# Front of an attention-plus-Fourier kernel: both row groups of a product accumulate into one bank, the upper one 17 products behind

## The chip, the cores and the metric

The kernel runs on one core of a Trainium2 chip. The time is the device time of the core in microseconds (us), from the first to the last instruction of an execution and what lies around it; lower is better. The engines are TensorE (PE, with its weight loads as PEld), VectorE (DVE), ScalarE (ACT), GpSimd (POOL) and SyncE (SP), which here only issues transfers. TensorE writes to PSUM, which has 128 partitions and eight banks of 512 four-byte numbers each; a product of 512 columns fills one bank.

## The reference

For x of 2048 by 512 the kernel gives `g * a + (1 - g) * b`:

```python
g = sigmoid((x * gate_w).sum(-1, keepdims=True))
# a: full attention, 32 heads of 16, softmax over 2048 keys
qkv = x @ wqkv                       # 512 -> 3 * 512
p = softmax(q @ k.T * 16 ** -0.5)
a = concat_heads(p @ v) @ wo
# b: real part of a Fourier transform over both axes
b = dft_seq_re @ (x @ dft_hid_re.T) - dft_seq_im @ (x @ dft_hid_im.T)
```

The weights wqkv and wo are large (64 times 0.05), so the softmax is sharp and the kernel works with operands split into a high part, rounded to the matrix format, and a low part, the rest. A product is then three products of parts: high by high, high by low, low by high.

## The kernel before

The program has two stages, and each writes its own order of instructions by hand; no scheduler moves them.

**The front** (about the first 365 us) makes five sets of products of x: q, k, v (with wqkv) and the real and imaginary parts of the transform over the hidden axis (called wr and wi after their weights). Each set has 16 output blocks of 128 by 512, so there are 80 blocks. `products` (L301 to L307) runs the 12 products of a block: four slices of 128 of the contracted axis, each with the three products of parts. `halves_of` (L185 to L189) issues a product as two matmuls of 64 rows, one on the lower and one on the upper half of TensorE's rows (the row groups); they run side by side and write to two banks. A block thus ends with two banks, whose sum is the result. The order of blocks is: q and k in turn, for the first 128 columns with one block of q beside them (blocks 0 to 8), the rest of q, the rest of k (to block 31), v (32 to 47), wr (48 to 63), wi (64 to 79).

`project_t` (L368) closes a block of q or k: ScalarE copies the first bank to `tx` (L380); while the scans have not begun, VectorE adds the second bank to it, later ScalarE copies the second bank too (L384) and GpSimd adds the two. Then ScalarE makes the high part `eh`, GpSimd subtracts it to make the low part `el` (both under L245, the line of the helper that runs due work), and SyncE stores both. `project_s` (L399) closes a block of v, wr or wi: ScalarE copies both banks (L406, L407), and GpSimd adds them (L478 for v, L502 for wr and wi, whose sums are stored).

Between the products stand **scans**: the kernel needs the row maxima of the scores of 16 pairs of heads, and the front does the first five pairs, 64 scans each. A scan is two matmuls of 48 rows (one on each row group), each into a bank of its own. The 64 scans of the first pair are plain: VectorE reduces each bank (L298). The 256 scans of the other four are folded (`scan_folded`, L150 to L165): of two adjacent blocks of keys, ScalarE takes the rectified first (L162) and VectorE adds the second and reduces (L164, a custom instruction and a short read of its accumulator). The second matmul of a folded scan is issued one scan later than the first.

Pace and due work hang on a count of slots, one slot per product. `beside` (L255) is called after each product: it raises the count, runs whatever `after(n, ...)` has put down for this slot, and issues scans by a running sum: 3.9 products for each plain scan, `FOLD_PACE` = 2.08 for each folded one. The scans begin 62 slots after block 8 has been issued (slot 170 of 960), when eight loads, put down from 22 slots after block 8, have brought the first pair's rows back from memory.

Eight banks serve this: four tags in two pairs for the blocks (x0, x1, y0, y1; before the scans the first blocks use the scan banks too), four for the scans (d0, k0 on the lower row group, d1, k1 on the upper; d for even scans, k for odd). A bank is reused when its reader is done.

**The main stage** (the rest) runs attention, the transform over the sequence axis and the remaining scans on eight other tags, in macro steps written out in `ORDERS`. The change does not touch it.

Of the kernel before, what the change touches and what calls it, by code (L numbers as in the profile page):

```python
# [10 lines left out]
F32 = mybir.dt.float32  # L11
# [7 lines left out]
P = 128  # L19
# [18 lines left out]
FOLD_PACE = 2.08  # L38
# [3 lines left out]
OUTM = 234  # L42
SCAN_MACROS = 226
# [14 lines left out]
def build(tc, x, xT, wqkv, wo, wrT, wiT, cr, ci, gate, out):  # L58
    nc = tc.nc
    with ExitStack() as ctx:  # L60
# [87 lines left out]
        fold = [None, None]  # L148

        def scan_folded(n, j, bank):  # L150
# [6 lines left out]
            b, ps = 64 * j, bank(f"{'dk'[c % 2]}{j}")  # L157
            nc.tensor.matmul(ps, qs[b:b + 48, qb * P:(qb + 1) * P], ks[b:b + 48, c * 512:(c + 1) * 512],  # L158
                             start=True, stop=True)
            if c % 2 == 0:  # L160
                fold[j] = cw.tile([P, 512], F32R, tag=("chi", "clo")[j], name="fold").bitcast(F32)
                nc.scalar.activation(fold[j], ps, AF.Relu)  # L162
            else:
                nc.vector.tensor_tensor_reduce(out=fold[j], in0=ps, in1=fold[j], scale=1.0, scalar=-3.0e38,  # L164
                                               op0=ALU.add, op1=ALU.max, accum_out=mx[p][:, j, qb, c // 2:c // 2 + 1])  # L165
# [55 lines left out]
        with ExitStack() as px:  # L221
            psf = px.enter_context(tc.tile_pool(name="psf", bufs=1, space=PSUM, reuse_waits="tile"))
            turns = [1]

            def narrow(tag, name="s"):
                return psf.tile([P, 512], F32, tag=tag, name=name)

            def xy(a=None):
                turns[0] += 1
                a = a or ("x", "y")[turns[0] % 2]  # L230
                return narrow(a + "0", "xy"), narrow(a + "1", "xy")
# [23 lines left out]
            def beside():  # L255
# [6 lines left out]
                while seen[0] < FRONT and pace[1] >= 1.0:  # L262
# [8 lines left out]
                    if n not in FOLDED:  # L271
                        done = scan_plain(n)
                    else:

                        scan_folded(n, 0, narrow)
                        done = behind(n - 1)
# [7 lines left out]
            def behind(n):  # L284
                if n in FOLDED:
                    scan_folded(n, 1, narrow)
                    return n

            def scan_plain(n):
# [4 lines left out]
                for j in range(2):  # L294
                    ps, b = narrow(f"{'dk'[n % 2]}{j}"), 64 * j
                    nc.tensor.matmul(ps, qs[b:b + 48, i // 4 * P:(i // 4 + 1) * P],
                                     ks[b:b + 48, i % 4 * 512:(i % 4 + 1) * 512], start=True, stop=True)
                    nc.vector.tensor_reduce(mx[p][:, j, i // 4, i % 4:i % 4 + 1], ps, axis=AX.X, op=ALU.max)  # L298
                return n

            def products(ps, parts):  # L301
                n = 0
                for lhs, rhs in parts:
                    for a, b in ((0, 0), (0, 1), (1, 0)):
                        halves_of(ps, lhs[a], rhs[b], n == 0, n == 3 * len(parts) - 1)
                        n += 1
                        beside()  # L307
# [10 lines left out]
            def split_operand(s, raw, engine):  # L318
                ah[s], al[s] = block(2 * s), block(2 * s + 1)
                split(ah[s], al[s], raw, engine)  # L320


            if True:
# [44 lines left out]
                def project_t(w, dst, f, c, ps=None):  # L368
                    ps = ps or xy()
                    products(ps, [([w[i][d][:, f * P:(f + 1) * P] for i in range(2)], xs[d, c])  # L370
                                  for d in range(ND)])
                    tx = ep.tile([P, 512], F32, tag="tx", name="tx", bufs=1)
                    folded = dst is k_d and f < 2
                    if folded and c % 2 == 0:
                        s = even[0] = rp.tile([P, 512], F32, tag="raw", name="ke")
                    else:
                        s = ep.tile([P, 512], F32, tag="ty", name="s")
                    hi = ep.tile([P, 512], F32R, tag="eh", name="eh", bufs=3)
                    lo = ep.tile([P, 512], F32R, tag="el", name="el")
                    nc.scalar.copy(tx, ps[0])  # L380
                    if pace[0] is None:
                        after(5, nc.vector.tensor_add, s, ps[1], tx)
                    else:
                        nc.scalar.copy(s, ps[1])  # L384
                        after(5, nc.gpsimd.tensor_add, s, s, tx)
# [6 lines left out]
                    if folded and c % 2:  # L392
                        after(10, fold_keys, f, c - 1, even[0], s)
                    after(9, nc.scalar.copy, hi, s)
                    after(10, nc.gpsimd.tensor_sub, lo, s, hi.bitcast(F32))
                    after(14, store, 0, hi)
                    after(20, store, 1, lo)

                def project_s(w, t, sign, use):  # L399
                    ps = xy()  # L400
                    q = slice((t % 4) * P, (t % 4 + 1) * P)
                    products(ps, [([v[:, q] for v in xs[d, t // 4]], [w[i][d] for i in range(2)])
                                  for d in range(ND)])
                    tx = ep.tile([P, 512], F32, tag="tx", name="tx", bufs=1)
                    ty = ep.tile([P, 512], F32, tag="ty", name="ty")
                    nc.scalar.mul(tx, ps[0], sign)  # L406
                    nc.scalar.mul(ty, ps[1], sign)  # L407
                    after(4, use, t, tx, ty)
# [29 lines left out]
                warm = [narrow("d0", "warm"), narrow("d1", "warm")]  # L438
# [13 lines left out]
                for n, (w, dst, f, c) in enumerate(order):  # L452
                    project_t(w, dst, f, c, xy("kxdykxdy"[n] if n < 8 else None))
                after(22, load_scan_beside, 0)
                after(62, scan_at, PACE)
                for f, c in [(2, 0), (3, 0)] + [(f, c) for f in range(1, ND) for c in range(1, NC)]:
                    project_t(wq, q_d, f, c)
                wv = new_w()
                for n, (f, c) in enumerate([(f, c) for f in range(1, ND) for c in range(NC)]):
                    if n == 1:  # L460
                        load_w(wv, wqkv[:, 1024:1536], 48, nc.gpsimd)
# [3 lines left out]
                wr = new_cw()  # L465
# [599 lines left out]
```

## Time and profile before

| | |
|---|---|
| median of the two runs | 1866.95 us (1866.27 and 1867.63) |
| profiled execution | 1860.47 us, span 1858.6 us |
| granted TensorE clock, mean | 0.99 |
| matmuls | 13640 |
| PE, DVE, ACT, POOL busy | 96%, 72%, 72%, 40% of the span |

The page gives each engine's busy time; the view by windows gives it for stretches of the span, with the number of instructions in brackets; the view of waits says which instruction ended an engine's idle time; the timeline lists instructions in order of time, with merged neighbours and their count. TensorE's matmuls are pipelined: one takes about 0.4 us from its start to its end, but the next starts about 0.23 us after it, so the pitch between starts, not the duration, is its price.

### The profile page before, as it was taken

What the parts mean: (1) busy time and instruction counts of PE and PEld (TensorE: products, weight loads), DVE (VectorE), ACT (ScalarE), POOL (GpSimd) and SP (SyncE); (2) the same over time, 40 slices, a digit from 0 to 9 for tenths busy, and PEclk for the clock granted to TensorE, in tenths of its full rate; (3) what the DMA queues carried; (4) which work ended last, traced back from release to release, by engine and by line L of the source; (5) the groups of instructions that cost most, each with busy time, mean ns of one, the idle gap of its engine ahead of it and who ended that gap; (6) DMA issues with size and microseconds to landing.
All of it is one profiled execution on the core that took longest, in us unless ns stands there. A gap on an engine that the chain in (4) does not pass through costs nothing.

```text
span 1858.6 us, 36455 instructions
## 1 busy us (share of the span) xinstructions
PE 1787.0 (96%) x13640; PEld 1043.2 (56%) x13640; DVE 1334.2 (72%) x2367; ACT 1331.1 (72%) x2583; POOL 752.1 (40%) x878
## 2 busy tenths in 40 slices
PE   8998899899999999999999899999999899999998
PEld 7776677655555555555555455555554455555554
DVE  6797788777777774886877677668876676684334
ACT  5449898877777777666677677776676677767785
POOL 3685433544444455333333334343333344333122
PEclk9999999999999999999999999999999999999999
DMA  8673325653643444334245644342423343515522
GB/s 280 210 234 90 86 84 124 157 136 101 131 109 87 114 119 119 79 73 85 69 89 122 192 92 91 77 98 71 104 67 67 85 88 79 104 50 131 184 51 94
DMA packets 130529, 205.37 MB, mean 110 GB/s; under 512 B 54336, under 2 KB 56880, under 8 KB 123632
## 3 DMA queue, kind: packets, MB, share of 16 engines
q1 hardware_dynamic: 90000, 176.23, 36.8%
q0 software_dynamic: 38496, 19.47, 4.6%
q10 hardware_dynamic: 1856, 7.34, 1.5%
q8 instruction: 107, 1.75, 0.4%
q14 instruction: 70, 0.57, 0.1%
HBM read 136.71 MB, written 65.81 MB: 109 GB/s over the span
## 4 chain that ended last, share of the span: by engine, by line
PE 77%; DVE 6%; ACT 4%; POOL 4%; DMA 3%; issue 3%; DVEq 0%; ACTq 0%; POOLq 0%; SPq 0%
PE pvb L603 24%; PE z L840 20%; PE s L624 15%; PE s L593 13%; PE xy L189 3%; PE s L158 3%; DVE mx L626 3%; DMA lc<-ob 2%; ACT fold L162 2%; POOL el L245 1%; POOL s L245 1%; DVE ob L633 1%; ACT ty L407 1%; ACT tx L406 1%; DVE y L753 1%
## 5 line engine op out<-in xcount | busy, mean ns | idle before, releaser
L626 DVE TENSOR_REDUCE mx<-s 128x1 f32<-128x512 f32 x1408 | 919.1, 686 | 246.5 <-PE s L593 136.2
L581 ACT ACTIVATE e<-s 128x512 f32<-128x512 f32 x1082 | 607.9, 605 | 210.1 <-PE s L593 167.9
L581 ACT ACTIVATE eb<-s 128x512 f32<-128x512 f32 x966 | 550.4, 605 | 208.3 <-PE s L593 163.5
L593 PE MATMUL s<-qs,ks 50*128 50x512 f32 x2048 | 688.5, 420 | 0.7
L840 PE MATMUL z<-b,chi 64*128 64x512 f32 x2060 | 594.6, 405 | 0.0
L624 PE MATMUL s<-ks,qs 48*128 48x512 f32 x1408 | 529.2, 456 | 27.9 <-DVE mx L626 23.4
L603 PE MATMUL pvb<-e,va 128*17 128x512 f32 x2164 | 473.1, 595 | 0.0
L603 PE MATMUL pvb<-eb,va 128*17 128x512 f32 x1932 | 462.4, 595 | 0.0
L593 PEld LDWEIGHTS s<-qs,ks 50*128 50x128 f32 x2048 | 358.1, 187 | 95.0 <-ACT e L581 27.5
L624 PEld LDWEIGHTS s<-ks,qs 48*128 48x128 f32 x1408 | 215.0, 185 | 331.1 <-DVE mx L626 140.7
L840 PEld LDWEIGHTS z<-b,chi 64*128 64x128 f32 x2060 | 333.8, 187 | 22.3
L840 PE MATMUL z<-b,clo 64*128 64x512 f32 x1030 | 342.5, 404 | 0.0
L215 POOL CAST chi<-craw 128x512 fp32r<-128x512 f32 x126 | 77.3, 613 | 434.5 <-PE z L840 341.4
L164 DVE CUSTOM_DVE_ANT_0 fold<-s,fold 128x512 f32<-128x512 f32 x256 | 172.2, 690 | 49.4 <-ACT fold L162 38.3
L840 PEld LDWEIGHTS z<-b,clo 64*128 64x128 f32 x1030 | 177.5, 188 | 10.8
L216 POOL TENSOR_TENSOR clo<-craw,chi 128x512 fp32r<-128x512 f32 x126 | 161.4, 1281 | 44.1 <-PE z L840 32.4
L636 POOL DMA_DIRECT2D lc<-ob x124 | 63.3, 516 | 273.6 <-DVE ob L633 267.6
L162 ACT ACTIVATE fold<-s 128x512 f32<-128x512 f32 x256 | 146.8, 605 | 21.8 <-PE s L158 12.1
L158 PE MATMUL s<-ks,qs 48*128 48x512 f32 x512 | 135.3, 421 | 22.0 <-ACT fold L162 20.6
L603 PEld LDWEIGHTS pvb<-e,va 128*17 128x17 f32 x2164 | 84.5, 97 | 125.2 <-issue 125.2
L603 PEld LDWEIGHTS pvb<-eb,va 128*17 128x17 f32 x1932 | 81.3, 96 | 106.9 <-issue 106.9
L189 PE MATMUL xy<-w,b 64*128 64x512 f32 x768 | 130.4, 395 | 0.0
(121 smaller groups left out, 1562.7 us busy)
## 6 DMA issues: line engine op xcount, KB each, us to landing
craw<-cr SPq DMA_DIRECT2D x64, 256.0 KB
craw<-ci SPq DMA_DIRECT2D x64, 256.0 KB
ks<-k_d SPq DMA_DIRECT2D x56, 256.0 KB
qs<-q_d SPq DMA_DIRECT2D x56, 256.0 KB
ab_d<-ab SPq DMA_DIRECT2D x32, 256.0 KB
y_d<-y SPq DMA_DIRECT2D x32, 256.0 KB
b<-bs_d SPq DMA_DIRECT2D x32, 256.0 KB
ks<-k_d SPq DMA_DIRECT2D x56, 128.0 KB
```

Source lines behind the costliest of these rows:

```text
L158: nc.tensor.matmul(ps, qs[b:b + 48, qb * P:(qb + 1) * P], ks[b:b + 48, c * 512:(c + 1) * 512], start=True, stop=True)
L162: nc.scalar.activation(fold[j], ps, AF.Relu)
L164: nc.vector.tensor_tensor_reduce(out=fold[j], in0=ps, in1=fold[j], scale=1.0, scalar=-3.0e38, op0=ALU.add, op1=ALU.max, accum_out=mx[p][:, ...
L189: nc.tensor.matmul(ps[j], lhs[r], rhs[r], start=first, stop=last)
L215: copy(hi, raw)
L216: sub(lo, raw, hi.bitcast(F32))
L581: nc.scalar.activation(e, ps, AF.Exp, scale=SCALE)
L593: nc.tensor.matmul(ps, ks[b:b + 50, kb * P:(kb + 1) * P], qs[b:b + 50, q0:q0 + 512], start=True, stop=True)
L603: nc.tensor.matmul(pvb[r:r + VC, :], va[:, kb, 2 * p + j, :], es[step][c, j], start=kb == 0, stop=kb == NB - 1, tile_position=(0, r))
L624: nc.tensor.matmul(ps, qs[b:b + 48, qb * P:(qb + 1) * P], ks[b:b + 48, c * 512:(c + 1) * 512], start=True, stop=True)
L626: nc.vector.tensor_reduce(mx[p][:, j, qb, c:c + 1], ps, axis=AX.X, op=ALU.max)
L840: nc.tensor.matmul(ps, pr_.lhs(j), pr_.rhs(j), start=group.count[j] == 1, stop=group.count[j] == group.size)
```

## The change

- A block now takes **one bank**. `products` issues only the matmul on the lower row group and puts the upper one into a list; once the list holds more than `LAG` = 17, `follow` issues the oldest. The upper group thus runs 17 products behind the lower one, into the bank that the lower one has already filled. At the end 17 upper matmuls are issued alone.
- The two groups must not write one bank at the same time. The **first upper matmul of a block waits** for the eviction (by ScalarE or VectorE) of a scan that was issued after the block's last lower matmul. Where no scans run, `mark` issues one: a matmul of 8 columns into a scan bank and a VectorE copy of one column.
- Banks: three for the blocks (p0 to p2), **five for the scans, in a ring**, whichever row group or parity a scan has.
- **One copy per block**. Before the scans begin ScalarE makes the high part straight from the bank and VectorE the low part; afterwards ScalarE copies the bank once and GpSimd makes both parts. For v, wr and wi ScalarE writes the final tile itself, and GpSimd's additions go. `split_operand` makes its high part on GpSimd, no longer on ScalarE.
- `FOLD_PACE` goes from 2.08 to 1.95 products per folded scan. The loads of the first pair start 30 slots (before: 22) after block 8, the scans 66 slots (62). Some buffers of weights are taken and split at other blocks.

Over the front this leaves ScalarE 106 instructions fewer (546 to 440) and GpSimd 48 fewer (152 to 104); VectorE has 18 short copies more and one addition fewer; TensorE 18 short matmuls more.

```diff
-FOLD_PACE = 2.08
+FOLD_PACE = 1.95
+LAG = 17
...
-            b, ps = 64 * j, bank(f"{'dk'[c % 2]}{j}")
+            b, ps = 64 * j, bank()
...
+            def product_bank():
+                turns[0] += 1
+                return psf.tile([P, 512], F32, tag=f"p{turns[0] % 3}", name="xy")
+            def scan_bank():
+                singles[0] += 1
+                return psf.tile([P, 512], F32, tag=f"s{singles[0] % 5}", name="s")
...
+            def mark(lhs, rhs):
+                ps = scan_bank()
+                issued[0] += 1
+                nc.tensor.matmul(ps[:, 0:8], lhs[0:64], rhs[0:64, 0:8], start=True, stop=True)
+                return nc.vector.tensor_copy(junk, ps[:, 0:1])
+            def follow():
+                ps, lhs, rhs, last, close = behind_.pop(0)
+                if ps.name in ends:
+                    at = ends.pop(ps.name)
+                    later = [ins for n, ins in marks if n > at]
+                    if not later:
+                        later = [mark(lhs, rhs)]
+                ins = nc.tensor.matmul(ps, lhs[64:P], rhs[64:P], start=False, stop=last)
+                if ps.name in starts:
+                    starts.remove(ps.name)
+                    if later:
+                        tc.add_manual_dep(ins.ins, later[0].ins.name, mybir.DependencyInfo(
+                            mybir.DependencyClass.Sync, mybir.DependencyReason.DATA), reason="row groups share a bank")
+                if last:
+                    close(ps)
-            def products(ps, parts):
-                n = 0
-                for lhs, rhs in parts:
-                    for a, b in ((0, 0), (0, 1), (1, 0)):
-                        halves_of(ps, lhs[a], rhs[b], n == 0, n == 3 * len(parts) - 1)
-                        n += 1
-                        beside()
+            def products(parts, close):
+                ps = product_bank()
+                pairs = [(lhs[a], rhs[b]) for lhs, rhs in parts for a, b in ((0, 0), (0, 1), (1, 0))]
+                for n, (lhs, rhs) in enumerate(pairs):
+                    nc.tensor.matmul(ps, lhs[0:64], rhs[0:64], start=n == 0, stop=False)
+                    issued[0] += 1
+                    if n == len(pairs) - 1:
+                        ends[ps.name] = issued[0]
+                        starts.add(ps.name)
+                        marks[:] = marks[-8:]
+                        if pace[0] is None or seen[0] >= FRONT:
+                            seen_by(mark(lhs, rhs))
+                    behind_.append((ps, lhs, rhs, n == len(pairs) - 1, close))
+                    if len(behind_) > LAG:
+                        follow()
+                    beside()
...
-                nc.scalar.copy(tx, ps[0])
-                if pace[0] is None:
-                    after(5, nc.vector.tensor_add, s, ps[1], tx)
-                else:
-                    nc.scalar.copy(s, ps[1])
-                    after(5, nc.gpsimd.tensor_add, s, s, tx)
+                    early = pace[0] is None
+                    if early:
+                        nc.scalar.copy(hi, ps)
+                        nc.vector.tensor_sub(lo, ps, hi.bitcast(F32))
+                    if not early or folded:
+                        nc.scalar.copy(s, ps)
+                    if not early:
+                        after(5, nc.gpsimd.tensor_copy, hi, s)
+                        after(6, nc.gpsimd.tensor_sub, lo, s, hi.bitcast(F32))
...
-                nc.scalar.mul(tx, ps[0], sign)
-                nc.scalar.mul(ty, ps[1], sign)
-                after(4, use, t, tx, ty)
+                    products(..., lambda ps: use(t, ps))
...
-                nc.gpsimd.tensor_add(va[:, t, :, 0:DH], tx..., ty...)
+                nc.scalar.copy(va[:, t, :, 0:DH], ps.rearrange("p (h e) -> p h e", e=DH))
...
-                        nc.gpsimd.tensor_add(ab, tx, ty)
-                        after(7, nc.sync.dma_start, ab_d[i][t], ab)
+                        nc.scalar.mul(ab, ps, (1.0, -1.0)[i])
+                        after(4, nc.sync.dma_start, ab_d[i][t], ab)
...
-                after(22, load_scan_beside, 0)
-                after(62, scan_at, PACE)
+                after(30, load_scan_beside, 0)
+                after(66, scan_at, PACE)
...
+                while behind_:
+                    follow()
+                    beside()
```

99 lines of the change are left out of this document (47 added, 52 removed).

## The prediction

> **What bounds the kernel now.** I read the page's busy shares first (they average over unlike stages), then the windows by stage (us from the start of the span; span of the window, then busy time and, in brackets, instructions of PE, PEld, DVE, ACT, POOL; then clock, DMA share and GB/s).
>
> ```profile
> 0.00:59.20 59.20, 49.50 (x367) 42.83 (x368) 32.95 (x52) 32.29 (x63) 22.97 (x23) 0.94 0.85 280
> 59.20:137.00 77.80, 77.79 (x622) 61.86 (x624) 75.00 (x125) 34.98 (x64) 60.57 (x48) 0.98 0.62 208
> 137.00:208.30 71.30, 60.00 (x466) 44.68 (x462) 52.89 (x157) 63.71 (x131) 39.43 (x32) 1.00 0.31 85
> 208.30:286.30 78.00, 72.95 (x572) 56.74 (x568) 63.09 (x193) 70.44 (x136) 28.06 (x22) 1.00 0.33 97
> 286.30:365.30 79.00, 73.33 (x564) 56.69 (x562) 62.40 (x189) 70.79 (x134) 33.21 (x26) 1.00 0.58 146
> 365.30:373.50 8.20, 5.52 (x31) 3.79 (x28) 6.22 (x12) 5.65 (x12) 4.87 (x5) 0.79 0.52 168
> 373.50:1858.60 1485.10, 1447.94 (x11034) 776.62 (x11032) 1041.68 (x1646) 1053.20 (x2047) 562.95 (x724) 0.99 0.41 98
> ```
>
> The rows are: products alone; plain scans; folded scans beside v (with the end of k), wr and wi; the passage to the main stage; the main stage. The last is untouched and TensorE is busy in 97.5% of it, so what the front saves comes off the end. In the folded stage ScalarE is busiest (about 90%), TensorE is not full. Who makes it wait, and how many scans a window holds (DVE, ACT), say the waits from 137.0 to 365.3 and the windows for the tile `fold`:
>
> ```profile
> PEld s L158 <- ACT fold L162: 39.0, 48, 1.6
> PEld s L158 <- DVE mx L164: 12.0, 54, 0.9
> ...
> DVE fold L164 <- ACT fold L162: 38.3, 41, 1.8
> ```
> ```profile
> 137.00:208.30 71.30, 49.48 (x73) 42.49 (x75) 1.00 0.31 85
> 208.30:286.30 78.00, 61.79 (x93) 52.87 (x93) 1.00 0.33 97
> 286.30:365.30 79.00, 60.86 (x92) 51.48 (x90) 1.00 0.58 146
> ```
>
> TensorE waits for a bank that ScalarE has not emptied, and VectorE waits for ScalarE as well. The timeline shows why:
>
> ```profile
> 208.75 0.59 ACT L406 ACTIVATE tx<-xy 128x512 f32<-128x512 f32 x1
> 209.22 0.61 ACT L407 ACTIVATE ty<-xy 128x512 f32<-128x512 f32 x1
> 209.70 0.64 ACT L475 ACTIVATE xg<-xg 128x512 f32<-128x512 f32 x1
> ...
> 210.31 2.29 ACT L162 ACTIVATE fold<-s 128x512 f32<-128x512 f32 x4
> ```
>
> The copies of a block (and in v's blocks a gate sum) stand together in ScalarE's queue: 0.47 + 0.48 + 0.61 = 1.56 us by the starts, in which no scan bank comes free.
>
> **Prices.** TensorE and VectorE, in a folded stretch, in the plain stage, and VectorE's two kinds of scan:
>
> ```profile
> 241.55 0.43 PE L158 MATMUL s<-ks,qs 48*128 48x512 f32 x2
> ...
> 242.29 0.40 PE L158 MATMUL s<-ks,qs 48*128 48x512 f32 x2
> ...
> 245.35 0.50 PE L158 MATMUL s<-ks,qs 48*128 48x512 f32 x1 [0.33 <-ACT fold L162]
> ```
> ```profile
> 65.28 0.60 PE L296 MATMUL s<-ks,qs 48*128 48x512 f32 x2
> 65.52 1.30 PE L189 MATMUL xy<-b,w 64*128 64x512 f32 x8
> 66.45 0.59 PE L296 MATMUL s<-ks,qs 48*128 48x512 f32 x2
> ```
> ```profile
> 83.73 8.45 DVE L298 TENSOR_REDUCE mx<-s 128x1 f32<-128x512 f32 x14
> ```
> ```profile
> 245.32 0.69 DVE L164 CUSTOM_DVE_ANT_0 fold<-s,fold 128x512 f32<-128x512 f32 x1 [0.86 <-ACT fold L162]
> 245.94 0.08 DVE L164 DVE_READ_ACCUMULATOR2_ANT mx<- 128x1 f32 x1
> 245.94 0.69 DVE L164 CUSTOM_DVE_ANT_0 fold<-s,fold 128x512 f32<-128x512 f32 x1
> ```
>
> Five pairs of matmuls (four products and a scan) take 66.45 - 65.28 = 1.17 us, so a pair (one on each row group) is 0.234 us; three pairs at 241.55 take 0.74, the same within 5%. A plain reduce is (8.45 - 0.69) / 13 = 0.597 us, a folded one 0.62 when its data is there.
>
> **The change, part by part.**
>
> *Folded stage.* Before, a block has 12 / 2.08 = 5.77 scans and costs TensorE 17.77 x 0.234 = 4.16 us, a scan 3.08 x 0.234 = 0.721. Measured: 71.3 / 74 = 0.963 us a scan beside v, 78.0 / 93 = 0.839 beside wr, and beside wi, where the last scan comes 2 us before the end, 77.0 / 91 = 0.846. The stalls are 1.40, 0.68 and 0.72 us a block. ScalarE's burst is 1.56 us beside v and 0.95 beside wr, so what the banks absorb is 0.16 to 0.27; I take 0.2. (Beside wi ten more casts stand on ScalarE, apart from the burst; the change moves them to GpSimd, busy for 33 of 79 us there.) Two things change. The burst loses a copy: 0.48 + 0.61 = 1.09 beside v, 0.48 beside wr and wi; GpSimd's additions, which came behind the copies, go too. And a bank comes back later: before every second scan, 2 x 0.721 = 1.44 us, in the ring after five scan matmuls, 2.5 scans of 2.95 x 0.234 = 0.690, so 1.73; 0.29 more, so 0.5 us is absorbed. Stall: 0.6 a block beside v, none beside wr and wi. At 1.95 a block has 6.15 scans and costs 18.15 x 0.234 = 4.25 us. The 256 scans span 499 products, 41.6 blocks: 12.7 up to the end of v, 28.9 after. Sum 12.7 x 4.85 + 28.9 x 4.25 = 184.4 us. Before it is 363.3 - 136.9, from the first and last start of its weight loads:
>
> ```profile
> L158 PEld LDWEIGHTS s<-ks,qs x512: 182/183/186, 136.9 to 363.3; 48*128 48x128 f32 x171
> ```
>
> 226.4 us, so **-42.0**. Bounds: no stall 41.6 x 4.25 = 177; nothing absorbed beyond 0.2, 12.7 x 5.14 + 28.9 x 4.53 = 196. I stand between, since both the burst and the ring are counted from rows. VectorE is not next: 256 x 0.62 = 159 us.
>
> *The wait of the first upper matmul.* It is new: the eviction of a scan issued after the block's last lower matmul. Queued behind it on TensorE is everything. Six products lie between, and in the folded stage three scans, six matmuls; the sixth needs the bank of the first in a ring of five anyway. So the wait adds about nothing to the ring's; taken at 0 here. In the plain stage only three scan matmuls lie between, and VectorE is the bound: 2 x 0.597 = 1.194 us a scan against TensorE's 4.9 x 0.234 = 1.15. After the wait two or three reduces are still queued (1.2 to 1.8 us), and the next scan comes after at most 3.9 products (0.9 us) and a matmul (0.4). From both sides: nothing, or one reduce (0.6) a block; I take 0.1 for 21 blocks, nearer to nothing for that queue.
>
> *Plain stage.* 64 x 1.194 = 76.4, with the 2.1 us of that wait 78.5, against 136.9 - 59.2 = 77.7: **+0.8** (-1.3 to +11).
>
> *Before the scans.* The stage ends on the first pair's loads, and GpSimd waited for a store before it could write `el` again:
>
> ```profile
> 59.21 0.60 PE L296 MATMUL s<-ks,qs 48*128 48x512 f32 x1 [3.93 <-DMA qs<-q_d]
> ```
> ```profile
> 44.79 0.65 SPq L124 DMA_DIRECT2D ks<-k_d  x1
> ...
> 52.10 0.42 SPq L124 DMA_DIRECT2D qs<-q_d  x1
> ```
> ```profile
> POOL el L245 <- DMA q_d<-el: 12.3, 3, 4.5
> ```
>
> Block 8 ends 17 slots later, but is split straight from the bank and stored 9 to 12 slots after, so its last store moves from slot 128 to 137 and the loads, on SP's queue behind it, by 8 slots: 8 x 0.23 = **+1.8 us**; TensorE, which waited 3.9 us for them, comes to the first scan four slots (0.9 us) later, so it still waits. Below: -2.1 (the faster rival). Above: `el` is now written by VectorE, so the 12.3 us of waiting for stores move there, with the marks behind them in its queue, and TensorE behind the marks and behind the bank that `el` is read from. That bank is needed 20 slots (4.7 us) after the store is issued, the mark 25 slots after, a little more than the longest wait (4.5), so I count it at nothing; without that cover up to +7.
>
> *Drain.* Scans start at slot 174 and take 250 + 499 products, to slot 923; products last to 960 and the upper group's 17 to 977. 54 slots at 0.234 are 12.6 us; before, 365.3 - 363.3 = 2.0. **+10.6**: the faster pace of scans is paid back here.
>
> *Passage.* Before, the work after the last scan falls on the first reduces of the main stage:
>
> ```profile
> 366.38 1.02 DVE L181 CAST chi<-mt 128x32 fp32r<-128x32 f32 x1
> ...
> 367.43 1.20 DVE L182 TENSOR_TENSOR clo<-mt,chi 128x32 fp32r<-128x32 f32 x1
> ...
> 369.81 0.18 PEld L624 LDWEIGHTS s<-ks,qs 48*128 48x128 f32 x1 [3.04 <-DVE mx L626]
> ```
>
> 3.0 us of waiting and, at a clock of 0.79 over 8.2 us, 1.7 more. With the last scan 12 us earlier that work is done: I take **-3.8** (-4.8 to 0: the last bank's copy and GpSimd's last split remain).
>
> *Sum*: -42.0 + 0.8 + 1.8 + 10.6 - 3.8 = -32.6 us. The profiled execution took 1860.5 us, so 1827.9 for it; the median of the runs is 1866.95, 6.5 above, and against it 1866.95 - 32.6 = 1834.
>
> **Two rules beside the rows.** The early splits, all 16 as a group, beside GpSimd's work:
>
> ```profile
> L311 DVE TENSOR_TENSOR b<-raws,b 128x512 fp32r<-128x512 f32 x16 | 14.9, 936 | 7.1 <-ACT b L310 7.1
> ```
>
> 936 ns each, against 690 for VectorE's folded scans above, which take one operand from a bank; the sum leaves them as they are. The Trainium skill, SBUF — State Buffer, section Who interferes with whom, says that a VectorE instruction with two SBUF inputs contends with a GpSimd instruction that reads SBUF; by that rule, which the row agrees with, the change takes most of GpSimd's reading out of this stage, the splits gain 3.9 us in all, and the sum gives 1830.
>
> Against the change: each block now waits once, at 0 to 0.1 us by the count of scans above. The Trainium skill, TensorEngine Tiling (Array Packing), section Restrictions and Gotchas, says that different row tiles can't access the same PSUM bank at once and that software must keep them apart, so the wait can't be left out. No run here shows such a collision; by the rows the wait is covered and the sum stays at 1834, and where it isn't, the slower rival holds.
>
> **The rivals.**
>
> *Faster.* Bursts are absorbed wholly (177, -49.4), and the early splits, 16 x (0.936 - 0.690) = 3.9 us too long beside GpSimd's low parts, run at 690 ns because VectorE now makes the low parts, from the bank: 1.8 - 3.9 = -2.1. With -1.3, +10.6 and -4.8 the sum is -47: 1820 us. For it speaks that VectorE waits for ScalarE and hardly for anything else. Against it: with 6.15 scans at 0.56 us (2.29 for four, less one's tail) and 1.09, ScalarE beside v needs 4.53 of 4.25 us.
>
> *It doesn't do what it says.* The ring mixes engines, so a late ScalarE now holds VectorE's matmuls too, and the stalls per block stay at 1.40 and 0.68: 12.7 x 5.65 + 28.9 x 4.93 = 214, -12; sum -3: 1864 us. The 38.3 us of VectorE waiting for ScalarE speak for it, the copy taken from each burst against it.
>
> *Slower.* The wait of the first upper matmul stops both row groups, in 62 blocks beside scans. If the awaited eviction stands behind a burst and VectorE and ScalarE run dry meanwhile, it costs on top of the ring. Break-even is 32.6 / 62.4 = 0.52 us a block; at 1.0 us the time is 1834 + 62 = 1896. Against it stands the count of six scan matmuls.
>
> **How the numbers follow.** Forecast 0.60, faster 0.20, no effect 0.12, slower 0.08. The forecast's own range is 1822 (177, -45) to 1857 (early +7, plain +4, fold 196, passage 0: -10). The range for 8 in 10 is 1819 to 1858: the faster rival inside, no effect and slower out. Two per cent (about what a measurement of this kernel can tell from no change) is 37 us, below 1829.6: the faster rival and a fifth of the forecast, 0.32. Slower by that needs (32.6 + 37.3) / 62.4 = 1.12 us a block: 0.03. Within: 0.65.
>
> **What would show it.** Right: TensorE's waits for `fold` from 51 to under 20 us; the folded scans within 177 to 196 us; about 12 us of products after the last scan; no 3 us wait at the main stage's first reduces; first scan near 61 us; VectorE's early splits shorter. Wrong: waits of L328 (the upper matmul) of 0.5 us a block; VectorE waiting for stores before 60 us with TensorE behind it; ScalarE still the cause of 30 us of waiting; or a main stage that changes by more than a few us.

## The result and the profile after

| | before | changed |
|---|---|---|
| median | 1866.95 us (2 runs) | 1834.40 us (2 runs, 1833.31 and 1835.50) |
| ratio | | 0.984, 95% interval 0.982 to 0.986 |
| profiled execution, span | 1860.47, 1858.6 us | 1835.50, 1833.7 us |
| PE, DVE, ACT, POOL busy | 1787, 1334, 1331, 752 us | 1782, 1327, 1271, 672 us |

The changed kernel is 1.6% faster, 26 to 34 us by the interval. The two profiled executions lie 24.9 us apart, since that of before was 6.5 us under its median; in the later comparisons, on other chips, the kernel before had medians of 1862.7 to 1863.3 us in 7 to 16 runs. So it is luck that the forecast of 1834 meets the median to the microsecond: its sum (-32.6) is 8 us more than the traces show, and the median that it starts from lies some 4 us above those of the other chips.

The windows of the changed kernel, cut at its own stages (columns as before: span, busy time and count of PE, PEld, DVE, ACT, POOL, clock, DMA share, GB/s):

```profile
0.00:60.20 60.20, 53.00 (x372) 42.58 (x372) 27.84 (x63) 25.98 (x52) 6.83 (x11) 0.94 0.79 263
60.20:141.40 81.20, 76.94 (x624) 60.98 (x623) 76.73 (x127) 15.89 (x28) 47.18 (x47) 0.98 0.67 222
141.40:200.30 58.90, 58.33 (x461) 41.55 (x459) 52.99 (x162) 55.24 (x118) 23.01 (x18) 1.00 0.32 85
200.30:272.50 72.20, 71.45 (x584) 54.38 (x584) 66.53 (x206) 63.63 (x126) 6.53 (x5) 1.00 0.40 111
272.50:331.30 58.80, 56.72 (x474) 43.91 (x472) 52.67 (x163) 49.05 (x93) 15.88 (x18) 1.00 0.66 159
331.30:344.00 12.70, 12.70 (x100) 11.54 (x97) 4.47 (x17) 4.01 (x7) 5.91 (x7) 1.00 0.54 168
344.00:352.00 8.00, 7.63 (x54) 5.69 (x53) 6.18 (x10) 7.16 (x15) 5.02 (x6) 1.00 0.49 146
```

The stage of products alone, the plain scans, folded scans beside v, wr and wi, a new row for the products after the last scan, and the start of the main stage, which no longer has the clock of 0.79. In the folded rows TensorE is now 96 to 99% busy (before: 84 to 94%). The folded scans run from 141.4 to 331.1 us, by their weight loads:

```profile
L165 PEld LDWEIGHTS s<-ks,qs x512: 182/184/188, 141.4 to 331.1; 48*128 48x128 f32 x171
```

That is 189.7 us instead of 226.4. Who still makes TensorE and VectorE wait, from 0 to 345 us (total, times, longest):

```profile
PEld s L165 <- DVE mx L171: 16.0, 59, 1.0
PEld s L165 <- ACT fold L169: 11.8, 34, 2.4
PEld xy L328 <- DVE mx L307: 7.8, 16, 1.5
PEld xy L344 <- DVE el L431: 4.1, 5, 1.8
```
```profile
DVE el L431 <- DMA q_d<-el: 8.6, 2, 4.7
DVE fold L171 <- ACT fold L169: 8.2, 21, 2.3
```

TensorE's waits for ScalarE fell from 39.0 to 11.8 us, VectorE's from 38.3 to 8.2; those of TensorE for VectorE rose from 12.0 to 16.0. The third row is the new wait of a block's first upper matmul (L328), for a plain reduce; for folded scans there is next to none. The `el` rows are the low parts that VectorE now makes before the scans.

From the front's marks the difference of the spans adds up (us; the stages before from its own rows):

| stage | forecast | before | changed | difference |
|---|---|---|---|---|
| up to the second scan matmul | +1.8 | 59.2 | 62.1 | +2.9 |
| plain scans, up to the first folded weight load | +0.8 | 77.7 | 79.3 | +1.6 |
| folded scans | -42.0 | 226.4 | 189.7 | -36.7 |
| from the last scan to the main stage (365.1 and 343.1) | +10.6 | 1.8 | 12.0 | +10.2 |
| from there to the end | -3.8 | 1493.5 | 1490.6 | -2.9 |
| sum | -32.6 | | | -24.9 |

The row of the main stage is the least certain: in the fourteen profiles of this document that stage, which no edit touches, took 1486.7 to 1494.9 us. Its start, up to the first weight load for `pvb`, can be told apart: 12.9 us before (365.1 to 378.0), 9.5 us now (343.1 to 352.6).

### The profile page after: what moved, and what is told of

It is laid out like the page before. It is cut to its first block, busy times and chain, and to the rows that moved or that the text cites. A ratio compares the mean times of both kernels' runs of the same rounds, so it can differ in the third digit from the quotient of the medians.

```text
span 1833.7 us, 36228 instructions
## 1 busy us (share of the span) xinstructions
PE 1781.7 (97%) x13658; PEld 1036.1 (57%) x13658; DVE 1326.6 (72%) x2384; ACT 1270.8 (69%) x2477; POOL 671.6 (37%) x830
## 4 chain that ended last, share of the span: by engine, by line
PE 82%; DVE 9%; DMA 5%; issue 2%; POOL 1%; ACT 1%; SPq 0%; DVEq 0%; ACTq 0%; POOLq 0%
PE pvb L648 24%; PE z L885 20%; PE s L669 15%; PE s L638 13%; PE xy L328 4%; PE xy L344 4%; DVE mx L307 4%; PE s L165 4%; DMA lc<-ob 3%; DVE mx L671 2%; DVE ob L678 1%; POOL lc L681 1%; DVE y L798 1%; DMA ab_d<-ab 1%; DMA y_d<-y 0%
## 5 line engine op out<-in xcount | busy, mean ns | idle before, releaser
L669 PE MATMUL s<-ks,qs 48*128 48x512 f32 x1408 | 528.1, 456 | 22.5 <-DVE mx L671 18.0
L171 DVE CUSTOM_DVE_ANT_0 fold<-s,fold 128x512 f32<-128x512 f32 x256 | 168.0, 689 | 17.4 <-ACT fold L169 8.2
L165 PE MATMUL s<-ks,qs 48*128 48x512 f32 x512 | 168.0, 405 | 3.4 <-ACT fold L169 2.5
L169 ACT ACTIVATE fold<-s 128x512 f32<-128x512 f32 x256 | 140.8, 605 | 18.8 <-PE s L165 18.3
L344 PE MATMUL xy<-w,b 64*128 64x512 f32 x384 | 121.2, 404 | 0.0
```

Source lines behind the costliest of these rows:

```text
L169: seen_by(nc.scalar.activation(fold[j], ps, AF.Relu))
L171: seen_by(nc.vector.tensor_tensor_reduce(out=fold[j], in0=ps, in1=fold[j], scale=1.0, scalar=-3.0e38, op0=ALU.add, op1=ALU.max, accum_out= ...
L344: nc.tensor.matmul(ps, lhs[0:64], rhs[0:64], start=n == 0, stop=False)
```

## The experiments

The ratios are to the kernel before on the same chip. "Fold" is the time from the first to the last weight load of the folded scans, read from the row of the scan tile in the one profile of each run (before 226.4, changed 189.7); "clock" is the granted TensorE clock over that time (before and changed 1.00). The changed kernel ran on the first chip alone, twice, so totals are set against its 1834.4 us across chips, and a few microseconds between totals carry little.

| run | median, us (runs) | ratio to before, 95% interval | fold, us | clock |
|---|---|---|---|---|
| e1 old kernel, pace 1.95 | 1863.86 (10) | 1.001 (0.999 to 1.002) | 222.4 | 0.99 |
| e2 changed, pace 2.06 | 1835.71 (4) | 0.986 (0.983 to 0.988) | 194.2 | 0.99 |
| e3 changed, two copies | 1850.46 (6) | 0.993 (0.991 to 0.995) | 205.3 | 1.00 |
| e4 changed, four scan banks | 1843.13 (4) | 0.989 (0.987 to 0.992) | 194.5 | 0.99 |
| e5 changed, both undone | 1855.54 (7) | 0.996 (0.995 to 0.997) | 209.8 | 1.00 |
| e6 changed, 14 behind | 1862.59 (10) | 1.000 (0.998 to 1.001) | 203.0 | 1.00 |
| e7 changed, 20 behind | 1844.55 (4) | 0.991 (0.988 to 0.993) | 194.2 | 0.99 |
| e8 changed, more buffers | 1834.53 (4) | 0.985 (0.982 to 0.988) | 187.1 | 1.00 |
| e9 changed, casts on ScalarE | 1840.30 (4) | 0.988 (0.986 to 0.990) | 193.9 | 0.98 |
| e10 changed, gate sum at the copy | 1840.01 (4) | 0.988 (0.986 to 0.991) | 191.6 | 1.00 |
| e11 changed, early blocks by GpSimd | 1843.21 (4) | 0.990 (0.988 to 0.992) | 193.5 | 0.98 |
| e12 changed, gate sums earlier | 1839.50 (4) | 0.987 (0.985 to 0.989) | 187.3 | 0.99 |

A clock under 1.00 is one stretch at 0.50 beside wi, 3.4 us long (6.8 in e9 and e11). My estimate is that it costs at most half of the time that TensorE was busy in it: 1.7 us in e1, e2, e4 and e7, 1.5 in e12, 2.3 in e9, 2.9 in e11. The changed kernel's fold has none, so beside it these are too long by up to that much.

The theory is the prediction's: a block stalls TensorE by ScalarE's burst of copies, less what the scan banks absorb. Its rivals are that the pace, the banks alone or the copies alone did it, that ScalarE's work as a whole sets the stage, however it is spread, and that the new wait costs what it saves.

**e1, the old kernel with the new pace.**

```diff
-FOLD_PACE = 2.08
+FOLD_PACE = 1.95
```

> The kernel before with one number changed: 1.95 products per folded scan instead of 2.08. Theory 'burst and banks' (a block stalls TensorE by ScalarE's burst of copies less what the scan banks absorb): the stalls per block stay at 1.40 us beside v and about 0.7 beside wr and wi, while a block now holds 6.15 scans and costs 4.25 us, so the folded stage takes 12.7 x 5.65 + 28.9 x 4.95 = 215 us instead of 226; some 41 products (9.6 us) then come after the last scan instead of 2 us; the wait at the passage to the main stage (3 us) goes. In all 7 us less: about 1860. Rival 'pace' (the gain of the change is mostly that scans end earlier): 20 us or more off, below 1847. Rival 'ScalarE is full': a folded scan takes its 0.88 us whatever the pace, the folded stage stays at 226 and the drain is added: about 1872.

The fold fell by 4.0 us (5.7 but for the stretch at half clock), and the products after the last scan took 9.5 us instead of 1.8: no difference in all. "Pace" is out. "ScalarE is full" is not: the fold (222.4) lies nearer to its 226 than to the theory's 215, with ScalarE busy for 200.0 us of it (90%, as before), while the total lies nearer to the theory. So the stalls per block, which the theory had held fixed, grew with the scans in a block. Nor did the start of the main stage get shorter, though the scans ended sooner: 12.8 us up to `pvb`, with these waits of TensorE and a clock of 0.87:

```profile
PEld s L624 <- DVE mx L626: 1.9, 2, 1.4
PEld s L593 <- ACT tx L406: 1.8, 1, 1.8
```
```profile
367.40:380.20 12.80, 10.15 (x61) 6.65 (x57) 7.59 (x12) 9.81 (x20) 9.33 (x11) 0.87 0.56 177
```

The wait for the reduces (3.0 us before) is down to 1.4, but one for ScalarE's copy of the last block's bank, which stands where it did, has come up.

**e2, the changed kernel with a slower pace.**

```diff
-FOLD_PACE = 1.95
+FOLD_PACE = 2.06
```

> The changed kernel with 2.06 products per folded scan instead of 1.95 (2.08 itself would let the last scan meet the first splits for the main stage). Theory 'burst and banks': 256 scans now span 527 products, 43.9 blocks of 11.83 x ... = 17.83 pairs, 4.17 us, with the stalls measured in the changed kernel (0.5 us a block beside v, 0.25 later): 12.7 x 4.67 + 31.2 x 4.42 = 197 us against 189.7; the drain after the last scan is 26 slots, 6 us, against 13. The two cancel, the total is within 3 us of the changed kernel: 1834 to 1838. Rival 'pace': if the gain hung on the pace, it comes out 10 us or more slower, 1844 and up.

As the theory had it in direction: 4.5 us more in the fold (expected 7), 6.5 us less after it (339.6 - 334.1 = 5.5 instead of 12.0). The pace moves time between the two and hardly changes their sum.

**e3, two copies per block.** In `project_t` (after the scans have begun) and `project_s`:

```diff
+    nc.scalar.copy(ep.tile([P, 512], F32, tag="tx", name="tx", bufs=1), ps)
     nc.scalar.copy(s, ps)
```

> The changed kernel, but after the scans have begun ScalarE copies each block's bank twice, first into a tile that nobody reads: the burst is as long as before the change, the five scan banks in a ring stay. Theory 'burst and banks': the burst is 1.57 us beside v and 0.96 later, the ring absorbs 0.5, so the stalls are 1.07 and 0.46 us a block and the folded stage takes 12.7 x 5.32 + 28.9 x 4.71 = 204 us, 14 above the 189.7 of the changed kernel: about 1848. Rival 'banks alone': the copy does not matter, within 4 us of 1834. Rival 'copies alone': the whole gain of the folded stage goes, 215 us, about 1860.

The fold took 205.3 us, 15.6 above the changed kernel (expected 14). TensorE's waits in the same view:

```profile
PEld s L165 <- ACT fold L169: 25.6, 54, 1.0
PEld s L165 <- DVE mx L171: 18.8, 62, 1.0
```

The waits for ScalarE more than double (11.8 before this edit), at the same count of banks. "Banks alone" is out; over 41.6 blocks the second copy costs 0.375 us each, most of its 0.48.

**e4, four scan banks.**

```diff
-            b, ps = 64 * j, bank()
+            b, ps = 64 * j, bank(f"{'dk'[c % 2]}{j}")
...
-                return psf.tile([P, 512], F32, tag=f"s{singles[0] % 5}", name="s")
+                return psf.tile([P, 512], F32, tag=tag or ("d0", "d1", "k0", "k1")[singles[0] % 4], name="s")
...
-                    ps, b = scan_bank(), 64 * j
+                    ps, b = scan_bank(f"{'dk'[n % 2]}{j}"), 64 * j
```

> The changed kernel, but the scans use four banks by row group and parity, as before the change; the fifth is left idle. One copy per block stays. Theory 'burst and banks': 0.2 us absorbed instead of 0.5, stalls 0.89 us a block beside v and 0.28 later, the folded stage 12.7 x 5.14 + 28.9 x 4.53 = 196 us, 6 to 12 above the changed kernel: 1840 to 1846. Rival 'banks alone': the folded stage falls back to 215 us, about 1860. Rival 'copies alone': within 3 us of 1834. With four banks the wait of a block's first upper matmul is no longer implied by the ring as it was, so part of a loss may show as waits of the upper matmul.

4.8 us more in the fold, 0.115 us a block, and about 3.1 (0.075 a block) but for the stretch at half clock, where the theory had the ring absorb 0.29 a block. Neither "banks alone" nor "copies alone" (a total within 3 us of 1834, measured 1843) fits. The waits hardly differ from those with the ring:

```profile
PEld s L165 <- DVE mx L171: 16.2, 62, 1.0
PEld s L165 <- ACT fold L169: 12.0, 35, 2.3
```

**e5, both undone.** The edits of e3 and e4 together.

> The changed kernel with both suspected causes undone at once: ScalarE copies each block's bank twice after the scans have begun, and the scans use four banks by row group and parity. The order of products, one bank per block, the pace of 1.95 and the work moved off ScalarE and GpSimd stay. In the runs with one of them undone the folded stage took 205.3 (two copies) and 194.3 (four banks) against 189.6 us. Theory 'burst and banks' (stall = burst less what the banks absorb, 0.2 with four): 1.37 and 0.76 us a block, 12.7 x 5.62 + 28.9 x 5.01 = 216 us, total about 1860. If the two only add: 189.6 + 15.7 + 4.7 = 210, about 1854. Rival 'something else' (the casts moved off ScalarE, GpSimd's additions, the staggered groups): with both undone the stage stays under 207 us, total under 1851, though the kernel before with the same pace took 222.2.

209.8 us: the two add (15.6 + 4.8 = 20.4, measured 20.1), and beside a second copy the ring is worth 4.5 (209.8 - 205.3, both at full clock). So the saving of 36.7 us in the fold splits into 4.0 for the pace (e1), 20.1 for copy and ring, and 12.6 for the rest (222.4 - 209.8), which e9 and e10 look for. With e1's stretch at half clock taken off, it is 5.7, 20.1 and 10.9.

**e6, the upper group 14 products behind.**

```diff
-LAG = 17
+LAG = 14
```

> The changed kernel with the upper row group 14 products behind instead of 17: three products and some three scan matmuls lie between a block's last lower matmul and the first upper one, instead of six and six. Theory 'covered wait' (at 17 the wait is implied by the ring): now it is not. The awaited eviction ends about 0.35 + 1.5 = 1.85 us after the block's end, the upper matmul is due after 4.6 x 0.234 = 1.1, so up to 0.8 us a block; as it also lets ScalarE and VectorE catch up, some of the 28 us of waiting for scan banks goes: folded stage 200 to 215 us, total 1844 to 1860, with waits of the upper matmul (L328) of 20 us or more there. Rival 'the wait is cheap anyway': within 3 us of the changed kernel.

The whole gain is gone, more than expected (1844 to 1860). Three products instead of six no longer cover the wait of the first upper matmul:

```profile
PEld xy L328 <- DVE mx L171: 13.8, 18, 1.0
PEld xy L328 <- DVE mx L307: 13.2, 16, 1.3
PEld xy L328 <- ACT fold L169: 13.2, 18, 1.9
```

27 us of waits in the folded stage, where the changed kernel has next to none, and 13.2 in the plain one; the fold is 13.3 us longer, the plain stage 10 us (63.0 to 154.8 against 59.9 to 141.4 by weight loads: 91.8 against 81.5), and its first scan comes 3 us later. The loss in the plain stage was not expected.

**e7, 20 behind.** `LAG = 20`, else as e6.

> The changed kernel with the upper row group 20 products behind instead of 17: nine products lie ahead of the first upper matmul, but only five, not eight, between a block's last upper matmul and the lower matmul that needs its bank. Theory 'covered wait': the waits of L328 for VectorE's reduces in the plain stage (7.8 us) go, without a gain, as VectorE bounds that stage; in their place waits of L344 for the block's copy: in the early stage 0.5 us a block (the bank is read by ScalarE and then VectorE), in the folded stage little. Drain three products longer (0.7 us). Total 0 to 8 us above the changed kernel: 1834 to 1842. Rival 'the wait costs': 5 us or more faster, below 1830.

A little worse than expected. The plain stage takes 145.3 - 69.4 = 75.9 us, VectorE's own bound (76.4), so in the changed kernel the wait costs there some 3 us (79.3). But the early stage pays more: its blocks' banks are read by ScalarE and then VectorE and come back late, and the first scan starts at 69.4 us. The fold, where little was expected, is 4.5 us longer (2.8 at full clock); in it TensorE waits 3.3 us for ScalarE's copies of blocks (L344), a wait that the changed kernel doesn't have.

**e8, more buffers.** A third buffer for `el`, a fourth for `eh` and the stored sums.

```diff
-                        lo = ep.tile([P, 512], F32R, tag="el", name="el")
+                        lo = ep.tile([P, 512], F32R, tag="el", name="el", bufs=3)
...
-                        ab = ep.tile([P, 512], F32, tag="eh", name="ab", bufs=3)
+                        ab = ep.tile([P, 512], F32, tag="eh", name="ab", bufs=4)
...
```

> The changed kernel with a third buffer for the low parts and a fourth for the tile that holds the high parts and, for wr and wi, the stored sums. It takes away two waits that the change moved onto VectorE and ScalarE: VectorE's for the store of a low part (8.6 us in two waits, one of which holds a mark and stops TensorE for 1.6 us at 56 us), and ScalarE's for the store of a sum (2.1 us at 318 us, with 2.4 us of TensorE behind it). Theory 'moved waits are on the path': the early stage 0 to 2 us shorter (the first pair's loads still set its end), the folded stage 2 to 4 us shorter: 1828 to 1832. Rival 'hidden': within 1.5 us of 1834.

The wait that it takes away stands in the changed kernel's timeline of ScalarE:

```profile
317.74 0.60 ACT L169 ACTIVATE fold<-s 128x512 f32<-128x512 f32 x1 [0.30 <-PE s L165]
320.43 0.60 ACT L543 ACTIVATE ab<-xy 128x512 f32<-128x512 f32 x1 [2.09 <-DMA ab_d<-ab]
```

ScalarE, which writes the sums itself now, waits for an older sum to be stored, and folds stand behind it. With the buffers the fold is 2.6 us shorter, as expected, and the early stage still ended on the loads (a wait of 4.4 us at the first scans), so its part was hidden. In the median the total isn't shorter, but the four runs lie in two pairs: 1830.9 and 1831.0 us, as the theory had it, at a mean clock of 0.990 and 0.991, and 1838.1 and 1839.8 at 0.987 (the changed kernel: 1833.3 at 0.991 and 1835.5 at 0.988). The profile is of a slower one and shows where its gain went: the products after the last scan took 14.3 us instead of 12.0, with 2.2 us of waits for marks, and the start of the main stage 12.1 us instead of 9.5, half of it at half the clock:

```profile
344.20:351.00 6.80, 6.80 (x29) 5.19 (x28) 2.77 (x4) 3.88 (x8) 3.49 (x6) 0.50 0.77 258
```

So the fold's gain is real, and whether the total keeps it ("moved waits are on the path") or not ("hidden") goes with the clock in these runs; the median of four doesn't settle it.

**e9, the casts back on ScalarE.**

```diff
-                engine.tensor_copy(ah[s], raw)
+                nc.scalar.copy(ah[s], raw)
```

> The changed kernel with one part undone: the high parts of the main stage's first operands (a cast of 128 x 512 in most blocks of wi) are made on ScalarE again, not on GpSimd. So far: with two copies and four banks the folded stage took 209.6 us, the kernel before with the same pace 222.2; 12.6 us are open. Beside wi a block took 4.92 and 5.30 us in those two, beside v 5.19 and 5.63, beside wr 5.03 and 5.12. Theory 'ScalarE's burst, casts too': each cast of 0.51 us stops the scans like a copy, so a block of wi goes from 4.49 to about 4.9 and the folded stage from 189.6 to 194 to 196 us; total 1838 to 1841. Rival 'GpSimd or the staggering': no difference, within 2 us.

The size is as expected (4.2 us in the fold), its cause only in part. ScalarE now waits for the operand's load, and in its longest wait (298.0 to 302.7 us) the clock falls:

```profile
ACT b L368 <- DMA abr<-ab_d: 5.9, 2, 4.7
```
```profile
301.70:308.50 6.80, 4.60 (x21) 3.51 (x23) 3.33 (x9) 4.76 (x9) 1.27 (x1) 0.50 0.82 273
```

TensorE's longest wait for a fold is 4.3 us (2.4 in the changed kernel). One stall of a load and the half clock that begins in it (up to 2.3 us) can make up most of the loss; how much the length of the casts does isn't told apart.

**e10, the gate sum at the copy.**

```diff
-                    after(7, lambda: nc.scalar.activation(xg, xg, AF.Copy, accum_out=z[:, t:t + 1]))
+                    after(10, lambda: nc.scalar.activation(xg, xg, AF.Copy, accum_out=z[:, t:t + 1]))
```

> The changed kernel with the gate sums of v's blocks on ScalarE three slots later, so that they stand with the block's copy in its queue, as they did before the change (there they stood right behind the two copies); now the copy comes three slots after the sum, because the upper row group ends a block 17 slots late. Theory 'length of the burst' (two jobs of 0.48 and 0.61 us a microsecond apart stall less than one of 1.09): a block of v goes from 4.67 to about 5.0 us (4.25 + 1.09 - 0.2 = 5.14 at most), the folded stage by 4 to 6 us to 194 to 196; total 1838 to 1841. Rival 'sum of ScalarE's work': no difference, within 2 us.

1.9 us in the fold instead of 4 to 6, at full clock in both, and 0.9 of them beside wr, which the edit leaves alone. So in the fold the rival, the sum of ScalarE's work, came out: whether the two jobs stand together matters little, that they are there matters more (e12). The total of 1840 isn't explained by the fold alone; in the profile 2.9 us of it stand in the main stage (1493.5 against 1490.6), which the edit doesn't touch.

**e11, the early blocks closed by GpSimd.** `early = False`.

> The changed kernel with the blocks before the scans closed as the later ones are: ScalarE copies the bank, GpSimd makes the high and the low part. VectorE then writes no low parts, so it waits for no stores, and GpSimd works beside VectorE's splits again. Theory 'loads set the end of this stage': the low part is there later (GpSimd needs 0.6 + 1.3 us, started 5 slots after the copy, its store 18 slots after instead of 12), so the first pair's loads come some 2 us later and the second scan matmul at 64 instead of 62.1 us; VectorE's splits take 0.85 to 0.95 us instead of 0.73, hidden; TensorE's waits of 3 us for VectorE's low parts and marks go without a gain. Total 0 to 4 us above the changed kernel. Rival 'VectorE's waits set it': 2 to 4 us shorter.

The total, 1843, is above the expected 1834 to 1838. The second scan matmul came at 65.1 us, 3 later, and the waits for VectorE's `el` were gone without a gain, as expected. The early splits, in the changed kernel and here:

```profile
L359 DVE TENSOR_TENSOR b<-raws,b 128x512 fp32r<-128x512 f32 x16 | 11.4, 731 | 6.0 <-ACT b L358 6.0
```
```profile
L359 DVE TENSOR_TENSOR b<-raws,b 128x512 fp32r<-128x512 f32 x16 | 15.2, 969 | 6.9 <-ACT b L358 6.9
```

The splits are the same instructions; only GpSimd's work beside them differs. The fold's 3.8 us more come with waits of ScalarE for stores of sums (3.5 us), the kind that e8 removes, and with the stretch at half clock (up to 2.9 us); the edit itself need not have a part in them.

**e12, the gate sums beside the plain scans.** One product on GpSimd and one sum on ScalarE per block, put beside blocks 15 to 30, in buffers of their own:

```diff
+                    after(16, nc.gpsimd.tensor_mul, xn, xn, gb)
+                    after(21, lambda: nc.scalar.activation(xn, xn, AF.Copy, accum_out=z[:, t:t + 1]))
...
```

> The changed kernel with the 16 gate sums (GpSimd's product, ScalarE's sum of 0.6 us) moved from v's blocks to blocks 15 to 30, beside the plain scans, where ScalarE is busy for 16 of 81 us and VectorE is the bound. Theory 'ScalarE's burst': a block of v then has only the copy, like one of wr, 4.5 instead of 4.67 us, so the folded stage is 2 to 4 us shorter (186 to 188); in the plain stage ScalarE's 10 us and GpSimd's 21 us are hidden behind VectorE, if GpSimd, at 47 of 81 us, keeps up. Total 1830 to 1832. Rival 'the plain stage has no room' (GpSimd late, so the stores and the loads of the next pair late): 3 us or more slower.

The fold fell to 187.3 us, inside the expected 186 to 188; beside v, up to wr's first weight load, it took 55.2 us instead of 58.8. But the plain stage took 2.8 us more (60.6 to 144.9 against 59.9 to 141.4), with 3.9 us of waits of TensorE for ScalarE's copies of blocks that the changed kernel doesn't have, and the total came out 5 us higher, as its rival had it. The gain was given back in the stage that was thought to have room. No run was faster than the changed kernel; e2 and e8 equal it.

## Why the prediction was right, and where it was not

The direction, the size and most stages were right; the terms differ as follows.

- **What bounded the folded stage** was right: ScalarE's copies among the folds. e3 shows it with one edit: a second copy brings back 15.6 of the 36.7 us, within 2 us of the figure that the theory gave. How a copy acts is less sure. The prediction priced it as a burst less what the banks absorb; e1 and e10 speak for ScalarE's work as a whole, and ScalarE is busy for nine tenths of the fold in all of these kernels (203.2 of 226.4 us before, 200.0 of 222.4 in e1, 186.0 of 205.3 in e3, 167.9 of 189.7 in the changed one). No run tells the two prices apart for the copy.
- **The step that was mis-sized is the ring.** The prediction let it absorb 0.29 us more of a burst, so that beside wr and wi nothing was left to stall. e4 measures 0.075 to 0.115 us a block. In the changed kernel a block of wr takes 72.2 / 16 = 4.51 us against TensorE's 4.25: 0.26 of stall with a burst of 0.48, so 0.22 are absorbed, as much as the prediction read off four banks. Why a fifth bank brings so little is not shown; the waits for VectorE's banks are 16.0 us with the ring and 16.2 without. Beside wr and wi the sum is 8.0 us too low by this (130.8 us, forecast 122.8).
- **Beside v** it is 2.7 us too high (58.9 us, forecast 61.6): the gate sum and the copy were taken as one burst, but they stand apart, though e10 gives that no more than 1.9 us. So two errors, one each way, left the fold 5 us off; that it came so near is in part luck.
- **The pace** is worth 4.0 to 5.7 us in the fold of the old kernel (e1), not the 11 that the same theory gave for it.
- **The rest of the fold**, 10.9 to 12.6 us that are neither copy, ring nor pace, has no term of its own in the sum. The prediction set the casts beside wi aside as "apart from the burst"; moving them back costs 4.2 us (e9), in part by a load that ScalarE then waits for and by the clock. Spacing the gate sum from the copy is worth up to 1.9 (e10). Some 7 us stay open, a good half of them beside v, where a block took 5.63 us with the old order at the new pace and 5.19 in e5. Waits of the old copies for GpSimd's additions, which are gone, are no candidate: in e1's folded stage ScalarE has no such wait, and before 1.4 us.
- **The new wait is covered**, as forecast, in the folded stage, by the six matmuls ahead of it; e6 shows that three are not enough, and that the slower rival's mechanism is real: at 14 products the change gains nothing. In the plain stage, where some had been counted, the forecast of 2 us stands against some 3 (e7).
- **The drain** (+10.6, measured +10.2) was right, and e1 shows it in the old kernel, where its 7.7 us take back more than the fold's 4.0.
- **The passage** (-3.8) was right in size: 3.4 us up to `pvb`, with the wait of 3.0 us and the low clock gone. Its reason, that the last scan ends earlier, is not enough: in e1 the last scan also ends well ahead, and the passage takes 12.8 us as before. What else the change does for it no run takes apart.
- **Before the scans** the loads set the end, as forecast, 2.9 us later instead of 1.8. VectorE's wait for a store, counted at nothing with little cover, did come up: a mark stood behind it and held TensorE:

```profile
57.99 0.49 PE L344 MATMUL xy<-b,w 64*128 64x512 f32 x1 [1.62 <-DVE junk L318]
...
62.10 0.47 PE L305 MATMUL s<-ks,qs 48*128 48x512 f32 x1 [1.54 <-DMA qs<-q_d]
```

It was hidden, since TensorE then waited 1.5 us for the loads anyway (e8, e11). The faster rival's rule held (splits of 731 ns instead of 936), but the time was not on the path.
- **A wait that was not foreseen**: ScalarE now writes the sums and waits for their stores, 2.1 us once, with TensorE's longest stall (2.4 us) behind it; e8 shows that the fold is 2.6 us shorter without.
- **One sign of being right** didn't come: TensorE's waits for the scan banks were to fall from 51 to under 20 us and fell to 27.8 (11.8 and 16.0). Two figures of the range don't come out of its terms, without effect on the forecast: with a fold of 177 they give -43.1, not -45, and at worst -8.8, not -10.

## What to carry to other kernels

Work on the engine that empties the banks is paid almost at full length when it stands among the evictions (0.375 of 0.48 us a block here); an extra bank in a ring shared by two engines bought a fifth to a third of what one copy less did. A wait that a new order forces is free only while enough independent work stands between cause and wait: 17 products gave a gain of 1.6%, 14 none, and 20 less again (0.9%), since the banks then came back late. Work moved to another engine takes its waits for transfers along, so look at what then stands behind it. Before a difference of a few microseconds between two profiles is put down to an edit, compare the granted clock of the stage in both.

## What the runs showed of the hardware

VectorE's subtraction with two SBUF inputs took 731 ns with little work on GpSimd and 936 to 969 ns beside GpSimd's splits, the same 16 instructions (before, changed, e11). This agrees with what the Trainium skill, SBUF — State Buffer, section Who interferes with whom, says of such pairs. TensorE's matmuls on the two row groups kept a pitch of 0.23 us a pair when the two belonged to different blocks and banks, as when they were halves of one product.

The granted clock fell to 0.50 for 3.4 or 6.8 us at a time, not at the same places in each profile: beside wi in e1 (from 324.4 us), e4 (324.7) and e9 (301.7), at the start of the main stage before (370.0), in e1 (372.2) and in e8 (344.2). Just ahead of it TensorE had waited 3.0 us before, 1.8 and 1.4 us in e1; the changed kernel's wait of 2.4 us in the fold was followed by none.
